# Spatial mixing by seven products of quarters, with x kept in DRAM for the z products and the projection as a stage of its own

## The chip, the core and the metric

One core of one Trainium2 chip runs the whole program. It has five engines with instruction streams of their own: TensorE (PE, matmuls, with weight loads shown as PEld), VectorE (DVE), ScalarE (ACT), GpSimd (POOL) and SyncE (SP, which here issues nearly all transfers). They meet through semaphores. The metric is the time on the device in microseconds (us); a kernel's time is the median of its runs.

## What is computed

x is 2048 x 512. The kernel computes x + s * silu(b), with s an attention over the last 512 keys of a cache and b a gated mixing unit; both take xn, the layer norm of x.

```python
def _A_ref(x, k_cache, v_cache, wq, wo):          # 32 heads of 128, W = 512
    q = (x @ wq)  ... per head
    p = _softmax(q @ k[-W:].T * Dh ** -0.5)
    return concat(p @ v[-W:]) @ wo

def _B_ref(x, w_in, w_sp, b_sp, w_out):           # F = 1376, Fh = 688
    z = _gelu(x @ w_in)
    z1 = z[..., :Fh]
    z2 = _layernorm(z[..., Fh:], axis=-1, eps=1e-5)
    g = einsum("ts,bsf->btf", w_sp, z2) + b_sp[None, :, None]
    return (z1 * g) @ w_out

xn = _layernorm(x)
out = x + _A_ref(xn, ...) * _silu(_B_ref(xn, ...))
```

The mixing is the product of w_sp (2048 x 2048) with the normalised z2 (2048 x 688). Everything is float32.

## The kernel before

A float32 matmul is done as three products of operands split in two: a high part (a cast to the matmul's float32 format, on ACT, called `wh`, `xh`, `z_h` and so on) and the rest (`rest`, L56: whole minus high, on DVE or POOL). `mm3` (L60 to 63) issues high x high, high x low and low x high into one PSUM bank. All of the program is written under a manual schedule: each engine works through its instructions in the order in which the code issues them, and waits in that order.

Rows of x are taken in 16 blocks of 128. The stages follow each other on TensorE:

1. A lead-in: layer norm of x, its transposed and split copy `xT` (L149 to L168), the first products.
2. The attention, 512 steps `t` (L372 to L411), four to each pair of head and quarter of the rows. A step issues scores, the q projection, the product with v and the output product, twelve 512-wide matmuls; each step sends its probabilities to DRAM (`p_dram<-pB`) and four steps' worth come back transposed (`pL<-p_dram`), and loads a piece of the weights (`raw<-wh`). The z1 half of `x @ w_in` and its way to DRAM lie in this stage as well. All these transfers are issued by SP in one order.
3. The z stage (L479 to L491): for each block two 344-wide halves of the z2 product (`z_product`, L448, 12 matmuls each), gelu on ACT and `bn_stats` on DVE (L457, L458), and for every two blocks the norm: aggregation (L464), the inverse root on POOL (`rsqrt`, L68 to L71) and two 688-wide `tensor_scalar` on DVE (L469). `z_split` (L472) makes high and low of z2, the low one on POOL. The 16 blocks of z2 stay in SBUF for the next stage. Within this stage the first w_sp block is loaded and split.
4. The mixing (L632 to L652): for each block i of output rows 16 chunks x 2 halves x 3 matmuls, 344 wide, into `ps_g` (`mix`, L557), while `take` (L541) loads and splits the w_sp pieces of the next blocks, cast on ACT and rest on DVE. Then `gate` (L568) adds the bias and multiplies by gelu of z1 (z1 comes from DRAM, its gelu is L638), `send_u` (L573) turns u in 32 x 32 squares on DVE and sends it through DRAM to get it transposed, `split_u` (L587) splits it, and `project` (L612) multiplies it with w_out, 17 matmuls of 512, one block behind the mixing. Silu, the product with s, the sum with x and the way out are L624 to L627. The last block is flipped by TensorE transposes (`flip_u`) instead of DRAM. ACT loads its tables anew each time it changes between gelu and silu.

The pools overlay each other in SBUF: z2 and the buffers of stages 3 and 4 take the memory of the attention.

## Time and profile before

| what | us |
| --- | --- |
| median of three runs (lowest, highest) | 1837.34 (1837.07, 1839.79) |
| the profiled execution | 1841.09 |
| its span | 1839.2 |
| z products begin, after the span's start | 1478.10 |
| mixing begins | 1536.98 |
| last mixing matmul begins | 1826.29 |

The profile is of one execution. Its page gives the busy time of each engine with its share of the span and the count of instructions; the chain that ended last, by engine; groups of equal instructions with their count, busy time and mean, and behind the last bar the idle time of the engine before them with what ended it; and the transfers with their size and the median time from issue to landing. An answer by windows has, for each stretch, the length, then the busy time of PE, PEld, DVE, ACT and POOL, the granted clock of TensorE, the busy share of the 16 DMA engines, and the GB/s that they moved. A row of the timeline has the start, the time that the row covers, engine, line, operation, output and inputs with their shapes, and the count; in brackets stands how long the engine had been idle, and what released it. The shown time of a single matmul includes its way through the array, so the distance between two starts is what counts.

### The profile page before, as it was taken

The numbers are of one execution on the slowest core, as the hardware profiler recorded it, in microseconds if no ns is written. First come the engines' busy times: TensorE is split into PE (matmuls) and PEld (weight loads), VectorE is DVE, ScalarE is ACT, GpSimd is POOL, SyncE is SP. The second block draws the span as 40 slices with busy tenths as digits, with TensorE's granted clock in tenths as the row PEclk, the third lists the DMA queues.
The fourth block names the chain that finished last, engine by engine and source line by source line (L and its number), as shares of the span: only waits on it lengthen the run. The fifth ranks groups of instructions, "written<-read, shape, count | busy, mean of one in ns | idle before, by whom it ended". The sixth has DMA issues, their size and how long they took to land.

```text
span 1839.2 us, 27426 instructions
## 1 busy us (share of the span) xinstructions
PE 1827.4 (99%) x8828; PEld 1573.1 (86%) x8828; DVE 1356.3 (74%) x2268; ACT 1019.4 (55%) x2188; POOL 873.6 (48%) x703
## 2 busy tenths in 40 slices
PE   8999999999999999999999999999999999999999
PEld 7888888888888888888888888888888999999998
DVE  7688888888888888888888888888888566333433
ACT  3566656666666665666666665665666445343422
POOL 3365555565565565555566555565566244000000
PEclk9999999999999999999999999999999999999999
DMA  5698888888888888888888888888888714554532
GB/s 190 179 234 216 217 219 224 215 218 218 221 214 217 216 219 217 216 214 217 219 224 217 218 216 226 215 218 217 218 215 225 222 65 153 174 184 140 182 120 91
DMA packets 404225, 369.69 MB, mean 201 GB/s; under 512 B 23056, under 2 KB 298768, under 8 KB 404080
## 3 DMA queue, kind: packets, MB, share of 16 engines
q1 hardware_dynamic: 399472, 362.30, 75.1%
q10 hardware_dynamic: 4608, 5.64, 0.9%
q8 instruction: 69, 1.13, 0.3%
q14 instruction: 76, 0.62, 0.1%
HBM read 213.70 MB, written 154.14 MB: 200 GB/s over the span
## 4 chain that ended last, share of the span: by engine, by line
PE 96%; DVE 1%; DMA 1%; ACT 1%; issue 0%; POOL 0%; ACTq 0%; SPq 0%; DVEq 0%; POOLq 0%
PE ps_a L61 14%; PE ps_a L62 14%; PE ps_a L63 14%; PE ps L63 13%; PE ps L61 13%; PE ps L62 13%; PE ps_g L61 4%; PE ps_g L62 4%; PE ps_g L63 4%; PE ps_f L63 1%; PE ps_f L62 1%; PE ps_f L61 1%; DMA z_dram<-z 0%; PE ps_f L621 0%; PE ps L166 0%
## 5 line engine op out<-in xcount | busy, mean ns | idle before, releaser
L57 POOL TENSOR_TENSOR pT_l<-pL,pT_h 128x512 fp32r<-128x512 f32 x507 | 658.6, 1299 | 572.1 <-ACT pT_h L256 526.2
L231 ACT ACTIVATE prob<-ps,nm 128x512 f32<-128x512 f32 x512 | 353.4, 690 | 533.6 <-DVE nm L229 531.5
L283 DVE SCALAR_TENSOR_TENSOR sacc<-ps,sums,sacc 128x512 f32<-128x512 f32 x496 | 370.7, 748 | 170.5 <-PE ps L63 170.4
L239 DVE STREAM_TRANSPOSE pB<-prob 128x512 f32<-128x512 f32 x512 | 359.4, 702 | 1.5 <-ACT pT_h L256 0.8
L229 DVE TENSOR_REDUCE nm<-ps 128x1 f32<-128x512 f32 x512 | 334.8, 654 | 3.6 <-PE ps L63 3.6
L256 ACT CAST pT_h<-pL 128x512 fp32r<-128x512 f32 x512 | 315.8, 617 | 7.6 <-ACT z L198 3.4
L61 PE MATMUL ps<-wh,qT_h 128*128 128x512 f32 x512 | 199.9, 390 | 0.9 <-DVE sacc L281 0.9
L63 PE MATMUL ps<-wh,oT_l 128*128 128x512 f32 x512 | 199.3, 389 | 0.3 <-DVE oT_l L57 0.3
L61 PE MATMUL ps_a<-xh,wh 128*128 128x512 f32 x512 | 199.4, 390 | 0.0
L62 PE MATMUL ps_a<-pT_l,wh 128*128 128x512 f32 x512 | 199.3, 389 | 0.0
L62 PE MATMUL ps_a<-xl,wh 128*128 128x512 f32 x512 | 199.3, 389 | 0.0
L62 PE MATMUL ps<-wl,qT_h 128*128 128x512 f32 x512 | 199.3, 389 | 0.0
L63 PE MATMUL ps_a<-xh,wl 128*128 128x512 f32 x512 | 199.2, 389 | 0.0
L63 PE MATMUL ps<-wh,qT_l 128*128 128x512 f32 x512 | 199.2, 389 | 0.0
L62 PE MATMUL ps<-wl,oT_h 128*128 128x512 f32 x512 | 199.2, 389 | 0.0
L61 PE MATMUL ps_a<-pT_h,wh 128*128 128x512 f32 x512 | 199.2, 389 | 0.0
L63 PE MATMUL ps_a<-pT_h,wl 128*128 128x512 f32 x512 | 199.2, 389 | 0.0
L61 PE MATMUL ps<-wh,oT_h 128*128 128x512 f32 x512 | 199.2, 389 | 0.0
L57 POOL TENSOR_TENSOR wl<-raw,wh 128x512 fp32r<-128x512 f32 (+1 forms) x132 | 169.6, 1286 | 37.0 <-ACT wh L120 37.0
L63 PE MATMUL ps_g<-z_h,xl 128*128 128x344 f32 x512 | 161.8, 316 | 0.0
L61 PE MATMUL ps_g<-z_h,xh 128*128 128x344 f32 x512 | 161.8, 316 | 0.0
L62 PE MATMUL ps_g<-z_l,xh 128*128 128x344 f32 x512 | 161.8, 316 | 0.0
(135 smaller groups left out, 2991.4 us busy)
## 6 DMA issues: line engine op xcount, KB each, us to landing
p_dram<-pB SPq DMA_DIRECT2D x512, 256.0 KB, 3.8
pL<-p_dram SPq DMA_DIRECT2D x512, 256.0 KB, 5.8
raw<-wh SPq DMA_DIRECT2D x128, 256.0 KB, 4.4
xh<-w_sp SPq DMA_DIRECT2D x32, 256.0 KB, 5.8
xl<-w_sp SPq DMA_DIRECT2D x28, 256.0 KB, 5.8
u_dram<-uB SPq DMA_DIRECT2D x15, 384.0 KB, 2.3
uL<-u_dram SPq DMA_DIRECT2D x60, 96.0 KB, 2.1
z_dram<-z ACTq DMA_DIRECT2D x32, 172.0 KB, 2.4
```

Source lines behind the costliest of these rows:

```text
L57: engine.tensor_tensor(lo, whole, hi.bitcast(F32), op=OP.subtract)
L61: nc.tensor.matmul(ps, lh, rh, start=first, stop=False)
L62: nc.tensor.matmul(ps, lh, rl, start=False, stop=False)
L63: nc.tensor.matmul(ps, ll, rh, start=False, stop=last)
L229: nc.vector.tensor_reduce(nm, ps, axis=AX.X, op=OP.max, negate=True)
L231: nc.scalar.activation(prob[t], ps, AF.Exp, bias=nm, accum_out=sums[b][:, j:j + 1])
L239: nc.vector.transpose(pB.rearrange("p (k q) -> p k q", q=Q), prob.pop(t))
L256: nc.scalar.copy(h, p)
L283: nc.vector.scalar_tensor_tensor(sacc[:, i, :], ps, rs, sacc[:, i, :], op0=OP.mult, op1=OP.add)
```

## The change

The mixing is written as a product of 2 x 2 quarters: w_sp is A11, A12, A21, A22 (each 1024 x 1024), z2 is B with row halves 1 and 2 and column halves of 344. Seven products of sums of quarters take the place of eight products of quarters, in the form that shares intermediate sums. For that, the z stage forms seven operands of each chunk: B11, B22, B21 and the sums T1 to T4, each as high and low, in one tile `ops`; the eighth chunk's lie in smaller buffers. Blocks p and p+8 are taken together. The sums of A are formed per pair of row blocks (i, i+8) on POOL. Each of the seven products of a pair takes 8 chunks x 3 matmuls of 344 into a PSUM bank of its own.

For these operands memory is needed that `xT` holds. So from step 32 to step 55 of the attention the blocks of `xT` that the z stage uses after its first two pairs are sent to `x_dram`, 256 KB each, and read back in the z stage (`load_xr`). u of all blocks goes to `u_dram`, and the projection follows the mixing as a loop of 16 blocks.

```diff
+    def keep_x(i, w):
+        g, j = divmod(i, 4)
+        nc.sync.dma_start(x_dram[:, i, w].rearrange("p (c t) -> p c t", c=NC), xT[g][w][:, :, j * P:(j + 1) * P].bitcast(F32))
+    STREAM = [p + a for p in range(2, H8) for a in (0, H8)]
+    KEEP = {32 + 2 * k + w: (i, w) for k, i in enumerate(STREAM) for w in range(2)}
...
             turn(t - 1)
+        if t in KEEP:
+            keep_x(*KEEP[t])
...
-            for k in range(2):
-                nc.vector.tensor_scalar(z[i - 1 + k], z[i - 1 + k], zmv[g][:, k, 0:1], r[:, k:k + 1],
-                                        op0=OP.subtract, op1=OP.mult)
+    T1, B11, B22, B21, T2, T3, T4 = range(7)
+    def z_norm(p, a):
+        for n in range(2):
+            h = z_half(p + a * H8, n)
+            nc.vector.scalar_tensor_tensor(h, h, zmv[p][:, a, 0:1], rz[p][:, a:a + 1].to_broadcast([P, NB]),
+                                           op0=OP.subtract, op1=OP.mult)
+    def whole(k, p):
+        if k == T3:
+            return R[3][:, p % 2 * NB:(p % 2 + 1) * NB]
+        return z_half(*{T1: (p, 0), B11: (p, 1), B22: (p + H8, 0), T2: (p + H8, 0),
+                        B21: (p + H8, 1), T4: (p + H8, 1)}[k])
+    def z_sums(p, which, engine):
+        for to, x0, x1 in which:
+            engine.tensor_tensor(whole(to, p), whole(x0, p), whole(x1, p), op=OP.subtract)
+    EARLY, LATE = ((T3, B22, T1), (T1, T1, B11)), ((T2, B22, T1), (T4, B21, T2))
+    def z_high(c, ks):
+        for k in ks:
+            nc.scalar.copy(op_of(k, c, 0), whole(k, c))
+    def z_low(c, ks, engine):
+        for k in ks:
+            rest(engine, op_of(k, c, 1), whole(k, c), op_of(k, c, 0))
...
+    ops = zp.tile([P, 7, H8 - 1, 2, NB], F32R, name="ops")
+    R = [zm.tile([P, H8 * P], F32, name=f"row{k}") for k in range(4)]
+    A_OF = (11, 12, 21, 22, 21, 11, 12)
+    B_OF = (B11, B21, T3, T4, T2, T1, B22)
+    def sum_a(m):
+        i, q = divmod(m, 7)
+        if i < H8 and q in (2, 4, 5, 6):
...
+            for h in range(2):
+                sl = slice(h * 512, h * 512 + 512)
+                nc.gpsimd.tensor_tensor(r[to][:, sl], r[x0][:, sl], r[x1][:, sl], op=op)
+    def split_a(m, engine=None):
...
+                nc.scalar.copy(hi, r)
+                rest(engine or nc.vector, lo, r, hi)
...
+    for p in range(1, H8):
...
+        for k, (i, n) in enumerate(order):
+            if p > 1:
+                z_product(i, n)
+            z_gelu(i, n)
+            if k == 0:
+                z_sums(p - 1, EARLY, nc.gpsimd)
+                z_high(p - 1, (B11, B22, B21))
+            elif k == 1:
+                z_low(p - 1, (B11, B22, B21), nc.vector)
+                z_sums(p - 1, LATE, nc.gpsimd)
+            else:
+                z_high(p - 1, ((T3, T1), (T2, T4))[k - 2])
+                z_low(p - 1, ((T3, T1), (T2, T4))[k - 2], nc.vector)
...
+            z_root(p, 0, 2)
+            z_norm(p, 0)
+            z_norm(p, 1)
...
+    z_norm(p, 0)
+    z_root(p, 1)
+    z_norm(p, 1)
+    z_high(p, (B11, B21, B22))
+    z_sums(p, EARLY, nc.vector)
+    z_low(p, (B11, B21, B22), nc.vector)
+    z_sums(p, LATE, nc.vector)
...
+    sum_a(2)
+    split_a(2)
+    z_high(p, (T4, T3))
+    z_low(p, (T4, T3), nc.vector)
+    load_row(0, 22, 3)
+    z_high(p, (T2, T1))
+    z_low(p, (T2, T1), nc.vector)
...
+        product(0, range(H8 - 1))
+        product(1, range(H8 - 1))
+        product(0, (H8 - 1,))
+        product(1, (H8 - 1,))
+        for m in range(M):
+            if m > 1:
+                product(m)
+            sum_a(m + 3)
+            if m:
+                split_a(m + 2)
+                outputs(m - 1)
...
+        for j in range(NT - 1):
+            project(j, M + j)
+            if j == 0:
+                outputs(M - 1)
+            split_u(j + 1)
+            load_u(j + 2)
+            load_sx(j + 2)
+            finish(j, M + j)
```

`outputs` adds the products' banks with the bias, multiplies by the gelu of z1 (`z1h`) and turns and sends u: about ten 344-wide DVE instructions and eight transposes for each pair of row blocks. `load_row` loads a quarter row of w_sp (512 KB) into one of four buffers; the fourth, `R[3]`, also holds T3 of the z stage until the last pair's is split. `load_u` fetches a block's u in four transfers, `load_sx` its s and x, `finish` is silu, product, sum and way out.

The order of DVE in the z stage, before, for two blocks (`stz` statistics, `mvz` mean and variance, `rz_r` the inverse root):

```order
L458 BN_STATS stz<-z 128x6 x2
L464 BN_AGGR mvz<-stz 128x2
L458 BN_STATS stz<-z 128x6 x2
L464 BN_AGGR mvz<-stz 128x2
L469 TENSOR_SCALAR z<-z,mvz,rz_r 128x688 x2
```

And now, for one pair of blocks (`blk` the halves of z2, `row_17556` the fourth row buffer with T3):

```order
L460 BN_STATS stz<-blk 128x6 x2
L60 TENSOR_TENSOR ops<-blk,ops 128x344 x3
L460 BN_STATS stz<-blk 128x6
L60 TENSOR_TENSOR ops<-row_17556,ops 128x344
L60 TENSOR_TENSOR ops<-blk,ops 128x344
L460 BN_STATS stz<-blk 128x6
L60 TENSOR_TENSOR ops<-blk,ops 128x344 x2
L467 BN_AGGR mvz<-stz 128x2 x2
L475 SCALAR_TENSOR_TENSOR blk<-blk,mvz,rz_r 128x344 x4
```

The rests of z2 have moved from POOL to DVE, seven 344-wide ones for the pair, and stand among the statistics of the pair that follows; the normalisation has become four instructions with a second tensor input.

POOL in the same place, now (first root, then the four differences of the pair):

```order
L73 TENSOR_SCALAR rz_t<-mvz 128x2
L74 TENSOR_TENSOR rz_r<-rz_t,power 128x2
L486 TENSOR_TENSOR row_17556<-blk 128x344
L486 TENSOR_TENSOR blk<-blk 128x344 x3
L60 TENSOR_TENSOR wl_18200<-row_17554,wh_18198 128x512
L60 TENSOR_TENSOR wl_18201<-row_17554,wh_18199 128x512
L73 TENSOR_SCALAR rz_t<-mvz 128x1
```

Before, the root was followed there by the 688-wide rests of z2. The last rows are those of the seventh pair, where two rests of w_sp come ahead of the last pair's root.

DVE behind the last pair's statistics, up to the mixing (`wl_` and `wh_` the splits of w_sp):

```order
L475 SCALAR_TENSOR_TENSOR blk<-blk,mvz,rz_r 128x344 x2
L486 TENSOR_TENSOR row_17556<-blk 128x344
L486 TENSOR_TENSOR blk<-blk 128x344
L60 TENSOR_TENSOR blk<-blk 128x344 x3
L486 TENSOR_TENSOR blk<-blk 128x344 x2
L60 TENSOR_TENSOR wl_18262<-row_17555,wh_18260 128x512
L60 TENSOR_TENSOR wl_18263<-row_17555,wh_18261 128x512
L60 TENSOR_TENSOR raw<-blk,raw 128x344
L60 TENSOR_TENSOR blk<-row_17556,blk 128x344
L60 TENSOR_TENSOR raw<-blk,raw 128x344 x2
L60 TENSOR_TENSOR wl_18172<-row_17556,wh_18170 128x512
L60 TENSOR_TENSOR wl_18173<-row_17556,wh_18171 128x512
```

`row_17556` is read for T3 by the ninth row from the top of this piece, and by the last two it holds the fourth quarter row of w_sp. Before, the mixing of a block needed only the pieces of one w_sp block, split in the z stage.

More of the change, by code (lines that the diff above doesn't have):

```diff
@@ L417, in mixer_kernel, with load_xr, z_half @@
     z1_out(NT - 1, 1, ps)
+    zst, zmv, rz, zps, xr, zbuf = {}, {}, {}, {}, {}, {}
+    def load_xr(i):
+        xr[i] = []
+        for w in range(2):
+            xr[i].append(rawp.tile([P, D], F32R, name="raw"))
+            nc.sync.dma_start(xr[i][w].bitcast(F32), x_dram[:, i, w])
+    def z_half(i, n):
+        if (i, n) not in zbuf:
+            if i % H8 == 0:
+                zbuf[i, n] = rawp.tile([P, 512], F32, name="raw")[:, :NB]
+            else:
+                zbuf[i, n] = zm.tile([P, HW], F32, name="blk", bufs=11)[:, :NB]
+        return zbuf[i, n]
@@ new lines, in z_product, with z_gelu @@
+    def z_product(i, n):
+        ps = zps[i, n] = ((ps_step.tile([P, 512], F32, name="ps_3") if i < H8 else
+                           ps_acc.tile([P, 512], F32, name="ps_a"))[:, :NB])
+        g, j = divmod(i, 4)
+        for c in range(NC):
+            x2 = (tuple(t[:, c, j * P:(j + 1) * P] for t in xT[g]) if i % H8 < 2 else
+                  tuple(t[:, c * P:(c + 1) * P] for t in xr[i]))
+            mm3(ps, c == 0, c == NC - 1, x2, cols(wt[("w", 2 + n), c], 0, NB))
+    def z_gelu(i, n):
+        if i not in zst:
+            zst[i] = stats.tile([P, 2, 6], F32, name="stz")
+        h = z_half(i, n)
+        nc.scalar.activation(h, zps.pop((i, n)), AF.Gelu_apprx_tanh)
+        nc.vector.bn_stats(zst[i][:, n, :], h)
```

415 lines of the change are left out of this document (217 added, 198 removed).

## The prediction

> **What bounds the kernel now.** I read the page first (busy shares, chain of waits), then busy time by windows, then the timeline of TensorE at the seams of the stages.
>
> ```profile
> span 1839.2 us, 27426 instructions
> PE 1827.4 (99%) x8828; PEld 1573.1 (86%) x8828; DVE 1356.3 (74%) x2268; ACT 1019.4 (55%) x2188; POOL 873.6 (48%) x703
> PE 96%; DVE 1%; DMA 1%; ACT 1%; issue 0%; POOL 0%; ACTq 0%; SPq 0%; DVEq 0%; POOLq 0%
> 100.00:800.00 700.00, 700.00 (x3090) 579.83 (x3089) 581.94 (x966) 427.74 (x965) 414.13 (x322) 1.00 0.87 218
> 1500.00:1550.00 50.00, 50.00 (x328) 50.00 (x327) 33.99 (x54) 26.84 (x49) 30.95 (x29) 1.00 0.27 88
> 1550.00:1600.00 50.00, 50.00 (x312) 48.67 (x311) 21.15 (x36) 18.68 (x25) 0.00 (x0) 1.00 0.64 210
> ```
>
> TensorE sets the time in every stage: no window has a gap, and the granted clock (the column after the five engines) is 1.00. So matmuls taken out pay in full as long as the other engines and the transfers keep up. The windows say how near they are: in the attention the transfers hold 0.87 of the DMA engines; in the z stage (1500 to 1550) DVE is busy 34 of 50 us and POOL 31; in the mixing (1550 to 1600) DVE 21 and POOL none. The change shifts work on all three.
>
> ```profile
> 1478.10 0.32 PE L61 MATMUL ps_a<-wh,xh 128*128 128x344 f32 x1
> 1536.98 0.32 PE L61 MATMUL ps_g<-z_h,xh 128*128 128x344 f32 x1
> 1540.66 0.32 PE L61 MATMUL ps_g<-z_h,xh 128*128 128x344 f32 x1
> 1826.29 0.32 PE L63 MATMUL ps_g<-z_h,xl 128*128 128x344 f32 x1
> 1827.37 0.39 PE L61 MATMUL ps_f<-wo_h,xh 128*128 128x512 f32 x1
> 1828.06 0.39 PE L61 MATMUL ps_f<-wo_h,xh 128*128 128x512 f32 x1
> ```
>
> The z products begin at 1478.10 and the mixing at 1536.98: 384 matmuls in 58.88 us, 0.1533 each. The two ps_g rows 3.68 us apart (24 matmuls) give the same. The ps_f rows, three matmuls apart, give 0.23 for a 512-wide one.
>
> **Matmuls removed.** The mixing had 16 x 16 x 2 x 3 = 1536; seven products of eight chunks for eight row pairs are 8 x 7 x 8 x 3 = 1344. 192 x 0.1533 = **-29.4 us**. The z stage keeps its 384, the projection its 16 blocks; six transposes go (1826.45 to the end is now 12.75 us, beside 14 projections of 17 x 0.23 inside; after, 15 x 3.9 and a tail of some 8.2): **-0.6**. All else hidden, that is 1837.3 - 30.0 = 1807.3.
>
> **The z stage.** Per pair p (blocks p and p+8) TensorE needs 48 x 0.1533 = 7.36 us. DVE had four bn_stats, two aggregations, two 688-wide normalisations per pair; it now has four bn_stats, two aggregations, four normalisations as two-input instructions and seven 344-wide rests, while POOL trades its two 688-wide rests for four 344-wide differences.
>
> ```profile
> L458 DVE BATCH_NORM_STATS2 stz<-z 128x6 f32<-128x344 f32 x32 | 15.9, 512 | 15.6 <-ACT z L457 15.1
> L464 DVE BATCH_NORM_AGGREGATE mvz<-stz 128x2 f32<-128x12 f32 x16 | 3.3, 209 | 0.5
> L570 DVE SCALAR_TENSOR_TENSOR u<-ps_g,bsp,z 128x344 f32<-128x344 f32 x32 | 17.0, 572 | 113.5 <-PE ps_g L63 113.5
> 1477.12 2.21 DVE L57 TENSOR_TENSOR wl<-raw,wh 128x344 fp32r<-128x344 f32 x5
> 1497.87 0.92 DVE L458 BATCH_NORM_STATS2 stz<-z 128x6 f32<-128x344 f32 x2
> 1472.80 0.93 POOL L57 TENSOR_TENSOR wl<-raw,wh 128x344 fp32r<-128x344 f32 x1 [6.65 <-ACT wh L120]
> 1487.00 0.22 POOL L70 TENSOR_SCALAR rz_t<-mvz 128x2 f32<-128x2 f32 x1 [13.27 <-DVE mvz L464]
> 1487.30 0.71 POOL L71 TENSOR_TENSOR rz_r<-rz_t,power 128x2 f32<-128x2 f32 x1
> 1488.05 1.19 DVE L469 TENSOR_SCALAR z<-z,mvz,rz_r 128x688 f32<-128x688 f32 x2 [1.14 <-POOL rz_r L71]
> ```
>
> DVE per pair: statistics 4 x 0.46 = 1.84, rests 7 x 0.44 = 3.09, aggregations 0.42, the wait for the root on POOL 1.14, normalisations 4 x (0.44, the subtract of that width, to 0.57, the gate from PSUM; I take 0.52) = 2.1. Together **8.6**, above TensorE's 7.36 before anything collides. POOL has 4 x 0.93 + 0.93 = 4.65, which would fit beside it, were the two independent. The trace says they are not:
>
> ```profile
> 1495.34 1.69 POOL L57 TENSOR_TENSOR z_l<-z,z_h 128x688 fp32r<-128x688 f32 x1
> 1495.41 2.54 DVE L469 TENSOR_SCALAR z<-z,mvz,rz_r 128x688 f32<-128x688 f32 x2 [1.14 <-POOL rz_r L71]
> 9.99 0.93 DVE L57 TENSOR_TENSOR pT_l<-pL,pT_h 128x344 fp32r<-128x344 f32 x2
> 15.28 1.70 DVE L57 TENSOR_TENSOR wl<-pL,wh 128x344 fp32r<-128x344 f32 x2 [0.51 <-ACT wh L120]
> 15.70 2.06 POOL L57 TENSOR_TENSOR wl<-pL,wh 128x344 fp32r<-128x344 f32 x2
> ```
>
> The pair of L469 that took 1.19 alone took 2.54 behind a POOL subtract of 1.69; two DVE subtracts that took 0.93 alone took 1.70 beside POOL's. The loser waits for the rest of the other's instruction. Rests and normalisations (11 of 17 DVE instructions) are of that kind, so POOL's 3.72 of differences can only lie under DVE's statistics (1.84); the root's wait is POOL's own. Period: 8.6 + 3.7 - 1.84 = **10.5**; bounds 8.6 (no collision) and 12.3 (no cover). [...]
>
> From 1478.10: pair 1's products end at 14.7 (its gelu must wait for them, as its buffers lie where the transposed x was), its normalisation at about 24 (25.7 with collisions), that of pair 6 five periods on, at 67 (78).
>
> **The start of the mixing.** Behind that stand, on DVE, pair 7's statistics, root twice (2.3), norms, two w_sp rests, then its own six differences, seven rests and more w_sp rests.
>
> ```profile
> L57 DVE TENSOR_TENSOR xl<-xh 128x512 fp32r<-128x512 f32 x33 | 21.1, 683 | 7.1 <-ACT xh L549 7.1
> L57 POOL TENSOR_TENSOR xl<-raw_z,xh 128x512 fp32r<-128x512 f32 x4 | 5.2, 1292 | 0.0
> L549 ACT CAST xh<-xh 128x512 fp32r<-128x512 f32 x33 | 18.7, 615 | 1.4 <-DMA xh<-w_out 1.4
> xh<-w_sp SPq DMA_DIRECT2D x32, 256.0 KB, 5.8
> ```
>
> TensorE can hide some under products 0 and 1, whose first seven chunks come early. But product 3 needs the fourth w_sp row, and its load waits on SP until DVE has done the rest of pair 7's T3, since that operand lies in the row's buffer. DVE up to there: 1.84 + 3.09 + 1.37 + 0.42 + 2.1 + 2.3 = 11.1; six differences and five rests 4.9; the half-rows' rests 1.37: normalisation of pair 6 + 16.5 to 17.3. Then the load (I take 4 of the 5.8; 512 KB on an idle queue), cast 0.62, rest 0.68: +21.5 to 22. POOL's last four differences and its two half-row rests (2 x 1.29) can add 5. Product 3 so starts at 67 + 21.5 = 88 (78 + 26.5 = 105), where TensorE alone would be at 58.9 + 3 x 3.68 = 69.9. **Lost: 18 without collisions, 35 with**; I take 35 (31 to 39), as the rows above show the collision for just these forms.
>
> **The rest of the mixing.** A row pair takes 7 x 3.68 = 25.8 us on TensorE. DVE: 14 rests x 0.68 = 9.5, some ten 344-wide additions and gates x 0.5 to 0.57, eight transposes: 16 to 18. POOL: 8 x 1.29 = 10.3. Even excluding each other, 9.5 + 10.3 is under 25.8. **0**; the cover is three sets of splits, two products ahead.
>
> **Saving x.** 24 transfers of 256 KB join SP's queue, one per attention step from 32 to 55, and return in the z stage (0.27 of the DMA engines taken there).
>
> ```profile
> p_dram<-pB SPq DMA_DIRECT2D x512, 256.0 KB, 3.8
> pL<-p_dram SPq DMA_DIRECT2D x512, 256.0 KB, 5.8
> raw<-wh SPq DMA_DIRECT2D x128, 256.0 KB, 4.4
> uL<-u_dram SPq DMA_DIRECT2D x60, 96.0 KB, 2.1
> ```
>
> A step of twelve 512-wide matmuls is 2.73 us and moves 218 GB/s at 0.87, so 262,144 bytes want about 1.05 us of the engines (218/0.87 = 250 GB/s) against 0.36 free: for 24 steps up to 16 us of transfers pile up. They delay p_dram and pL, which have slack of some steps. Bounds 0 and 9 us; I take **+2**, as the queue also holds weight loads that may slip.
>
> **The projection on its own.** Silu now comes without the table switches, off the path before too. At the seam, weights, outputs and the first u block pass DVE behind the last products: **+2.4** (0 to 5). Per block SP moves 384 + 512 + 256 KB, 1.18 MB in 3.9 us: 302 GB/s, against 210/0.64 = 328 at full. u is loaded two blocks ahead when its buffer comes free: landing 2.1, four issues, cast and rests about 5.2 + 2.1 for two periods of 3.9. At a landing of 3 or more it binds: **+2** (0 to 9).
>
> **Sum**: -29.4 - 0.6 + 35 + 2 + 2.4 + 2 = +11.4. The profiled execution took 1841.09 for its span of 1839.2, and the span alone lies 1.9 above the median of the runs, 1837.34; all terms are differences, so I add them to the median: 1848.7, say **1849**.
>
> **Rivals.**
> - *No exclusion between POOL's differences and DVE*: lost 18 in place of 35, and x saved free: -30.0 + 18 + 2.4 + 2 = -7.6 to -5.6: about 1831. For it: L458 ran at its own time beside POOL, and the trace has no 344-wide normalisation. Against it: the 1.70 and 2.54. It ends faster; the sign turns at a loss of about 24.
> - *Everything hidden*: 1807 to 1815. Against it: DVE's 8.6 against 7.36 alone costs 9.
> - *Saving x fills the queue*: with 9 in place of 2, and the projection bound by transfers (+9): about 1860.
> - *A slower clock after pauses.* TensorE would pause for 3 us in each pair.
>
> ```profile
> 10.00:20.00 10.00, 7.79 (x38) 6.79 (x38) 6.28 (x12) 2.94 (x7) 4.01 (x6) 0.84 1.05 393
> ```
>
> Where it paused, at the start, the clock was 0.84. At that, 7.36 becomes 8.8, still under 10.5; only the first products of the mixing would pay, 1 to 4 us: 1852. [...]
>
> **Chances.** Forecast (1840 to 1859) 0.55, no exclusion 0.21, full queues 0.13, clock 0.07, all hidden 0.04. Range **1830 to 1862**: 0.04 and part of the second lie below, 0.06 above. This kernel's times can tell about 0.2% (3.7 us) from nothing. Faster by more: most of the second, the fifth, a sliver of the first, 0.24; same 0.07; slower 0.69.
>
> **What would show it.** Right: in the z stage pairs some 10.5 us apart, subtracts on DVE of 0.8 to 1.4 beside POOL's; TensorE idle by some 35 us between 1478 and 1585, the last wait before the fourth product being the row's load; then products 3.68 apart. Wrong: pairs at 8.6 or less, subtracts at 0.44, or gaps in the attention between steps 32 and 60.

## The result, and the profile after

The changed kernel takes 1866.21 us (median of 4 runs, 1863.36 to 1868.53), the kernel before 1837.61 on the same chip (4 runs, 1837.07 to 1839.79). The ratio is 1.0153, 95% interval 1.0135 to 1.0170: slower, by 1.5%. The prediction said slower, by 11.4 us; it is 28.6 (27.5 between the spans of the two profiles). 1866 lies above the range.

The page of the changed kernel, its busy shares and the shares of the chain that ended last:

```profile
span 1866.7 us, 27811 instructions
PE 1823.3 (98%) x8630; PEld 1559.1 (84%) x8630; DVE 1495.7 (80%) x2496; ACT 1030.9 (55%) x2271; POOL 977.4 (52%) x784
PE 92%; DVE 3%; DMA 3%; ACT 1%; issue 1%; SPq 0%; POOL 0%; ACTq 0%; DVEq 0%; POOLq 0%
```

TensorE has 198 records fewer, as the 192 matmuls and six transposes ask. But its busy time fell by 4.1 us in place of 30: matmuls at a lower clock or a wider spacing count as busy too (from 1574.0 to 1578.7 it is busy for all 4.70 us at a granted 0.62). In the chain that ended last TensorE holds 92%, where it held 96%: the end now hangs, by these rounded shares for some 75 us more, on DVE, on transfers and on issue.

Windows through the z stage and the mixing (columns as before):

```profile
1520.00:1540.00 20.00, 19.86 (x125) 19.32 (x124) 16.79 (x35) 9.34 (x23) 10.39 (x12) 1.00 0.38 128
1540.00:1560.00 20.00, 4.67 (x22) 3.94 (x21) 16.80 (x34) 10.97 (x26) 11.10 (x13) 0.67 0.00 0
1560.00:1580.00 20.00, 16.20 (x69) 14.91 (x67) 15.34 (x26) 5.33 (x12) 8.54 (x14) 0.73 0.19 61
1600.00:1650.00 50.00, 50.00 (x319) 50.00 (x319) 41.55 (x63) 19.78 (x37) 22.63 (x16) 1.00 0.44 141
```

From 1520 to 1560 DVE is busy 16.8 of each 20 us, and what it stands idle it waits for the root and the gelu; between 1540 and 1560 TensorE has little to do, and until 1580 it runs at 0.7 of its clock. The last window looks perfect, 50.00 of 50 at full clock, and yet hides a loss: 319 matmuls in 50 us are one in 0.157, where the kernel before had 328 and 0.1533.

The timeline of TensorE in the changed kernel: first mixing matmul, the first of product 3, two rows 24 matmuls apart (3.78 us) behind it, and the seam to the projection.

```profile
1555.64 0.65 PE L64 MATMUL pm<-ops,wh 128*128 128x344 f32 x1 [13.33 <-ACT wh L553]
1579.34 0.43 PE L64 MATMUL pm<-ops,wh 128*128 128x344 f32 x1 [0.23 <-ACT wh L553]
1583.26 0.32 PE L64 MATMUL pm<-ops,wh 128*128 128x344 f32 x1
1587.04 0.32 PE L64 MATMUL pm<-ops,wh 128*128 128x344 f32 x1
1785.92 0.79 PE L64 MATMUL pm<-ops 128*128 128x512 f32 x1 [4.23 <-ACT ops L738]
1788.96 0.80 PE L66 MATMUL pm<-ops 128*128 128x512 f32 x1 [1.82 <-DVE ops L60]
```

The z products begin at 1478.74. Counted from there (T0), since T0 lies anywhere from 1473.9 to 1479.6 in the runs of this kernel and its edits, the time divides so. "No loss" is the 361.1 us that the kernel before took from its T0 to its end, less 30.0 for the work taken out.

| stretch | no loss | forecast | measured |
| --- | --- | --- | --- |
| start of the span to T0 | 1478.1 | 1480.1 | 1478.7 |
| T0 to product 3 | 69.9 | 104.9 | 100.6 |
| product 3 to the last mixing matmul (1781.38) | 194.9 | 194.9 | 202.0 |
| from there to the end | 66.3 | 70.7 | 85.3 |

The forecast was 4.3 us too high for the start of the mixing and 1.4 too high for saving x; it was 7.1 too low in the mixing and 14.6 too low behind it: 16.0 in all. That the two terms priced too high hid 5.7 of the 21.7 that were missing is luck. These two stretches are what the experiments had to settle, beside the start, which is the largest loss and may have come out right for a wrong reason.

### The profile page after: what moved, and what is told of

It reads as the page before. It is cut to its first block, busy times and chain, and to the rows that moved or that the text cites. A ratio compares the mean times of both kernels' runs of the same rounds, so it can differ in the third digit from the quotient of the medians.

```text
span 1866.7 us, 27811 instructions
## 1 busy us (share of the span) xinstructions
PE 1823.3 (98%) x8630; PEld 1559.1 (84%) x8630; DVE 1495.7 (80%) x2496; ACT 1030.9 (55%) x2271; POOL 977.4 (52%) x784
## 4 chain that ended last, share of the span: by engine, by line
PE 92%; DVE 3%; DMA 3%; ACT 1%; issue 1%; SPq 0%; POOL 0%; ACTq 0%; DVEq 0%; POOLq 0%
PE ps L64 13%; PE ps L66 13%; PE ps_a L66 13%; PE ps_a L64 13%; PE ps L65 13%; PE ps_a L65 13%; PE pm L66 4%; PE pm L65 4%; PE pm L64 4%; DVE ops L60 1%; DMA ops<-u_dram 1%; DMA raw<-x_dram 1%; DVE wl L60 1%; DMA z_dram<-z 0%; PE ps L188 0%
## 5 line engine op out<-in xcount | busy, mean ns | idle before, releaser
L285 DVE SCALAR_TENSOR_TENSOR sacc<-ps,sums,sacc 128x512 f32<-128x512 f32 x496 | 370.7, 748 | 169.2 <-PE ps L66 168.9
L545 POOL TENSOR_TENSOR row<-row,row 128x512 f32<-128x512 f32 x64 | 100.9, 1605 | 103.8 <-DMA row<-w_sp 69.5
L221 DVE SCALAR_TENSOR_TENSOR qT_l<-ps_a,qT_h 128x512 fp32r<-128x512 f32 x128 | 88.6, 692 | 67.7 <-ACT qT_h L220 67.7
L64 PE MATMUL pm<-ops,wh 128*128 128x344 f32 x392 | 127.5, 325 | 13.6 <-ACT wh L553 13.6
```

Of the source, the lines that this page charges most:

```text
L64: nc.tensor.matmul(ps, lh, rh, start=first, stop=False)
L221: nc.vector.scalar_tensor_tensor(lo, ps, SCALE, hi.bitcast(F32), op0=OP.mult, op1=OP.subtract)
L285: nc.vector.scalar_tensor_tensor(sacc[:, i, :], ps, rs, sacc[:, i, :], op0=OP.mult, op1=OP.add)
L545: nc.gpsimd.tensor_tensor(r[to][:, sl], r[x0][:, sl], r[x1][:, sl], op=op)
```

## The experiments

All are the changed kernel with an edit, if nothing else is said, and are compared by stretches from T0, since total times contain the spread ahead of it. What a stretch repeats to: where an edit leaves the start alone, product 3 comes between T0 + 100.4 and 101.0, and where it leaves the mixing's end and the projection alone (the first three runs below), these take 83.9 to 85.6.

### What sets the start of the mixing

**POOL's differences left out** (pairs 0 to 6):

```diff
             if k == 0:
-                z_sums(p - 1, EARLY, nc.gpsimd)
                 z_high(p - 1, (B11, B22, B21))
...
-                z_sums(p - 1, LATE, nc.gpsimd)
```

> Leaves out the four differences that POOL forms for each of the pairs 0 to 6 in the z stage (the operands T1 to T4 of these pairs are then plain blocks, so the output is not the reference's); everything else is kept. Theory (POOL's differences shut DVE's two-input instructions out): a pair takes 8.0 to 8.7 us in place of 10.0 (root to root on POOL), DVE's 344-wide rests fall from 0.69 to about 0.44 and the normalisations from 0.64 to about 0.51, the last pair's root comes 7 to 10 us earlier, and the whole is 6 to 10 us shorter. Rival (DVE's own work sets the pace, the pairs of slow instructions are chance): the pair stays at 10.0 and the time within 2 us.

The roots of pairs 1 and 6 and DVE's rests, first of the changed kernel, then of this run:

```profile
1501.50 0.71 POOL L74 TENSOR_TENSOR rz_r<-rz_t,power 128x2 f32<-128x2 f32 x1
1551.43 0.71 POOL L74 TENSOR_TENSOR rz_r<-rz_t,power 128x2 f32<-128x2 f32 x1
L60 DVE TENSOR_TENSOR ops<-blk,ops 128x344 fp32r<-128x344 f32 x36 | 23.4, 688 | 0.0
```

```profile
1500.40 0.71 POOL L74 TENSOR_TENSOR rz_r<-rz_t,power 128x2 f32<-128x2 f32 x1
1543.40 0.71 POOL L74 TENSOR_TENSOR rz_r<-rz_t,power 128x2 f32<-128x2 f32 x1
L60 DVE TENSOR_TENSOR ops<-blk,ops 128x344 fp32r<-128x344 f32 x36 | 17.8, 536 | 0.0
L475 DVE SCALAR_TENSOR_TENSOR blk<-blk,mvz,rz_r 128x344 f32<-128x344 f32 x28 | 16.4, 645 | 7.9 <-POOL rz_r L74 7.8
```

Five pairs take 49.9 us with POOL's work and 43.0 without: 10.0 and 8.60 a pair. A rest of unchanged size and operands takes 536 ns in place of 688. Product 3 comes at T0 + 91.1, 9.5 earlier. So the two engines do hold each other up, and the rival "no exclusion" is out; but POOL's differences cost 9.5 us, not the 17 between the prediction's two cases. The normalisations take as long without them (645 ns; 644 in the changed kernel, shown below), against the expectation of some 0.51 us: the differences read what the normalisations write and so come behind them, and of a pair's instructions only the rests are slowed by them (the statistics at 1517.25, wholly within a row of POOL's differences, took 0.51 us, and those at 1519.59, behind it, 0.51 too). The larger part of the 30.7 stays, 21.2: DVE's own work, the load of the fourth row, and POOL's work on w_sp, which this run keeps. The run took 1860.44.

**The normalisation as an instruction without a second tensor:**

```diff
-            nc.vector.scalar_tensor_tensor(h, h, zmv[p][:, a, 0:1], rz[p][:, a:a + 1].to_broadcast([P, NB]),
-                                           op0=OP.subtract, op1=OP.mult)
+            nc.vector.tensor_scalar(h, h, zmv[p][:, a, 0:1], rz[p][:, a:a + 1], op0=OP.subtract, op1=OP.mult)
```

> The normalisation as a tensor_scalar with two per-partition scalars in place of a scalar_tensor_tensor with a broadcast second input. Theory (DVE's two-input work and POOL's differences take turns and set the pace): a normalisation falls from 0.51 to about 0.30 (1.19 for 2 x 688 in the kernel before), a pair from 10.0 to 9.1 to 9.4, and the end by 4 to 6 us. Rival (the pair's pace is set by POOL's chain of root, differences and casts): the pair stays within 0.2 of 10.0.

The group in the changed kernel, then in this run:

```profile
L475 DVE SCALAR_TENSOR_TENSOR blk<-blk,mvz,rz_r 128x344 f32<-128x344 f32 x28 | 16.4, 644 | 7.8 <-POOL rz_r L74 7.8
```

```profile
L475 DVE TENSOR_SCALAR blk<-blk,mvz,rz_r 128x344 f32<-128x344 f32 x28 | 12.9, 521 | 7.9 <-POOL rz_r L74 7.8
```

The pairs take 9.51, a little above the 9.1 to 9.4 expected, and product 3 comes at T0 + 97.5: 3.1 us won by a form that computes the same. Four times the 0.12 us that an instruction got shorter is the 0.5 that a pair gains, so it is the instruction itself that is cheaper, no collision that went. The run took 1859.83; its span is 8.7 us shorter, but 4.7 of these lie ahead of T0, which this edit cannot reach: a reason to compare stretches.

**The clock kept up** by 78 + 36 matmuls whose results nobody reads:

```diff
+    dz = ps_step.tile([P, 512], F32, name="ps_3")
+    for _ in range(78):
+        nc.tensor.matmul(dz[:, :NB], op_of(B11, 0, 0)[:, :P], op_of(B11, 0, 0), start=True, stop=True)
...
+        bank(2)
+        for _ in range(36):
+            nc.tensor.matmul(banks[2][:, :NB], op_of(B11, 0, 0)[:, :P], op_of(B11, 0, 0), start=True, stop=True)
         product(0, (H8 - 1,))
```

> Adds 78 idle-filling matmuls (344 wide, their result unused) behind the last z product and 36 more ahead of the eighth chunks of products 0 and 1. Theory (the first products run at half clock because TensorE paused): the first products of the mixing follow each other at about 0.158 in place of 0.287, the granted clock between 1540 and 1580 rises from 0.67 and 0.73 to above 0.95, and the fourth product starts up to 6.5 us earlier. Rival (the chain on DVE and the load of the fourth row set the fourth product's start, and the slow matmuls only fill its wait): it starts at the same place to 1.5 us, with the wait ahead of it grown by what the products saved.

Two windows and the start of product 3 in this run:

```profile
1540.00:1560.00 20.00, 17.35 (x108) 16.78 (x107) 16.79 (x34) 11.21 (x26) 10.40 (x13) 0.97 0.00 1
1560.00:1580.00 20.00, 19.10 (x106) 18.81 (x104) 15.60 (x26) 4.63 (x11) 8.29 (x14) 0.86 0.15 46
1580.53 0.43 PE L64 MATMUL pm<-ops,wh 128*128 128x344 f32 x1 [1.43 <-ACT wh L553]
```

The clock rises from 0.67 and 0.73 to 0.97 and 0.86, DVE's busy time stays, and product 3 starts at T0 + 100.9. The slow matmuls at the start cost nothing: DVE's chain sets this start, not TensorE. Its last link here is the load of the fourth row: issued at 1575.98, when DVE is done with T3, landed at 1579.78, and the cast (`wh`) waits for it alone. In the changed kernel it was issued at 1575.04, and its cast, at 1578.67, is put down to TensorE's products 0 and 1, which end at 1578.65, most of their last stretch at half speed (0.287 apart up to 1577.46): there the two links come out together.

### The spacing in the mixing

**A pause in the kernel before.** One matmul ahead of the mixing of block 5 waits for a POOL instruction; all else is the kernel before.

```diff
+            if i == 5:
+                s3 = us[3, "x"][0]
+                nc.gpsimd.tensor_tensor(gap[:, :64], s3[:, :64], s3[:, 64:128], op=OP.subtract)
...
+                nc.tensor.matmul(us[5][0][:64, :64], gap[:, :64], gap[:, :64], start=True, stop=True)
```

> The kernel before, with one pause of TensorE of some 3 us ahead of the mixing of block 5 (a small matmul that waits for a POOL subtract of the third block's product with s). Theory A (a lead that the sequencer loses in a pause and wins back under 512-wide matmuls): the 96 matmuls of block 5 stand 0.158 apart, those behind the next projection 0.153 again, and the time grows by the pause, its slow clock if any, and 0.4 us. Theory B (a state after a pause): 0.158 from there to the end, some 960 matmuls x 0.0044 = 4.2 us beside the pause. Theory C (operands): 0.153 throughout.

```profile
1630.16 0.24 PE L641 MATMUL ps_g<-gap 128*64 128x64 f32 x1 [2.52 <-POOL gap L639]
1636.12 0.32 PE L61 MATMUL ps_g<-z_h,xh 128*128 128x344 f32 x1
1639.90 0.32 PE L61 MATMUL ps_g<-z_h,xh 128*128 128x344 f32 x1
1647.00 0.39 PE L61 MATMUL ps_f<-wo_h,xh 128*128 128x512 f32 x1
1651.36 0.32 PE L61 MATMUL ps_g<-z_h,xh 128*128 128x344 f32 x1
1655.04 0.32 PE L61 MATMUL ps_g<-z_h,xh 128*128 128x344 f32 x1
```

(This run took 1847.43. Narrow stands for 344 columns, wide for 512.) After a pause of 2.5 us 24 narrow matmuls take 3.78 us, as in the mixing of the changed kernel; behind the next projection, 17 matmuls of 512, they take 3.68 again. Operands and code are the same. So a pause alone slows narrow matmuls, by 2.7%, until wide ones have run.

The z stage of the changed kernel shows the same without an edit. Up to 1496.98 its 344-wide products stand 0.1533 apart; then one waits 2.0 us for a block of x, and from there on 24 take 3.79, with the same split of w_in (`wh`) as moving data:

```profile
1499.33 0.39 PE L64 MATMUL ps_a<-wh,raw 128*128 128x344 f32 x1 [2.03 <-DMA raw<-x_dram]
1503.63 0.32 PE L64 MATMUL ps<-wh,raw 128*128 128x344 f32 x1
1507.42 0.32 PE L64 MATMUL ps_a<-wh,raw 128*128 128x344 f32 x1
```

**Wide matmuls into the changed mixing**: 24 ahead of products 16 and 37, then 96 with changing weights ahead of product 16.

```diff
+            if m in (16, 37):
+                bank(m)
+                w = ring[m % 3][0][0]
+                for _ in range(24):
+                    nc.tensor.matmul(banks[m], w[:, :P], w, start=True, stop=True)
```

> Adds 24 matmuls of 512 columns (result unused) ahead of products 16 and 37 of the mixing. In the mixing of the changed kernel 344-wide matmuls stand 0.1577 apart, 0.1533 before TensorE's first pause at 1497. Theory A (the sequencer needs 0.158 for a pair of weight load and matmul, and the 0.153 of before is lived from a lead that wider matmuls rebuild): behind each block of 512-wide ones the spacing is 0.153 for some tens to some hundreds of matmuls, then 0.158 again. Theory B (a state that TensorE keeps after a pause) and theory C (where the operands lie): 0.158 throughout. The added blocks themselves are 2 x 24 x 0.228 = 10.9 us; A gives up to 3.3 of them back, B and C nothing.

> 96 matmuls of 512 columns with changing weights (result unused) ahead of product 16 of the mixing, where 24 with the same weights left the spacing of the 344-wide ones behind them at 0.158, while in the kernel before 17 of them had brought it back to 0.153. If it was their number or the repeated weights: 0.153 behind the block, for 50 matmuls or more. If the mixing itself holds 0.158 (where the operands lie, or the waits that stand at every twelfth matmul): 0.158 from the first one behind it. The time grows by 96 x 0.228 = 21.9 us, less up to 4.

In both the spacing stays at 0.158 behind the wide ones, so neither brought 0.153 back (1870.51 and 1884.57 us). The pause is not all of it.

**Probes.** Behind wide matmuls stand 48 narrow ones that read one fixed place as moving data, with nothing to wait for: in the first run the start of a w_sp split, an operand's high part, its low part; then places 0, 32, 64, 96, 128 and 192 bytes into a w_sp split; then the order 128, 0, 96, 0, 64, 0.

```diff
+                for o in (32, 0, 24, 0, 16, 0):
+                    for k in range(16):
+                        nc.tensor.matmul(banks[m], w[k // 4 % 2][:, k % 4 * P:k % 4 * P + P], w[k % 2], start=True, stop=True)
+                    for k in range(48):
+                        nc.tensor.matmul(banks[m][:, :NB], w[k // 4 % 2][:, k % 4 * P:k % 4 * P + P], w[0][:, o:o + NB], start=True, stop=True)
```

> Ahead of product 16 of the mixing, three times: 24 matmuls of 512 columns, then 48 of 344 columns without a wait among them (results unused); the 344 moving columns are, in turn, a split of w_sp, the high part of an operand in the tile of operands (its start a multiple of 64 bytes) and its low part (32 bytes further). If what holds the mixing at 0.158 is where its operands lie: 0.153 in the first run of 48, 0.158 in the third, perhaps in the second. If it is the waits at every twelfth matmul: 0.153 in all three, 0.158 again in the product behind. If it is a state that wider matmuls do not lift here: 0.158 in all three. The time grows by 72 x 0.228 + 144 x 0.155 = 38.7 us.

> Ahead of product 16 of the mixing, six times: 16 matmuls of 512 columns, then 48 of 344 (results unused) with one and the same tile as moving data, read from 0, 32, 64, 96, 128 and 192 bytes behind its start (the tile's own address is a multiple of 128 bytes). If the start of the moving data within 128 bytes sets the spacing: 0.153 at 0 and 128, 0.158 at 32 and 96, 0.160 at 64 and 192. If it is the tile of operands as such (its place in memory, or other engines' traffic there): 0.153 at all six. The time grows by 96 x 0.228 + 288 x 0.156 = 66.8 us.

> As the run with the offsets, but in the order 128, 0, 96, 0, 64, 0 bytes. If the start of the moving data decides: 0.153 in the second, fourth and sixth run of 48, and 0.157, 0.158, 0.156 in the first, third and fifth. If the order decides (a lead or state that the first run uses up): 0.153 in the first alone.

The third run's rows where 48 at 128 bytes begin, the wide ones behind them, 48 at 0, and the wide ones behind those:

```profile
1633.99 0.79 PE L775 MATMUL pm<-wh 128*128 128x344 f32 x4
1641.54 0.39 PE L773 MATMUL pm<-wh 128*128 128x512 f32 x1
1645.17 0.78 PE L775 MATMUL pm<-wh 128*128 128x344 f32 x4
1652.53 0.39 PE L773 MATMUL pm<-wh 128*128 128x512 f32 x1
```

7.55 us and 7.36. In all three runs the place decides, whatever the order: 7.36 at 0 bytes, 7.52, 7.49, 7.56, 7.55 and 7.68 at the others; 7.57 for the operand's high part and 7.68 for its low. The second run's theory, 128 bytes as fast as 0, failed with its 7.55, and so did its rival, 0.153 at all six.

**The place, in the mixing itself.** Products 3 to 48 read operands that lie at one chosen place modulo 256 bytes; the last of the three runs also has 24 wide matmuls ahead of product 16.

```diff
+        def rhs(m, k, c, w):
+            if not 2 < m < 49:
+                return op_of(k, c, w)
+            j = min(((k * 7 + min(c, 6)) * 2 + w) // 8 * 8 + 1, 97)
+            return ops[:, j // 14, j // 2 % 7, 1]
```

> Products 3 to 48 of the mixing (1104 matmuls) read as moving data only those operands of the tile that begin at a multiple of 16 x 1376 = 43 x 512 bytes from its start, in place of their own (so the output is not the sum of products that the reference asks for; count, width, weights and banks of the matmuls stay). Theory (where the moving data begin decides the 0.1575 spacing): these products run at 0.1533, 24 matmuls in 3.68 us, product 3 to product 49 in 169.3 us, and the mixing gets some 4.7 us shorter than the 202.0 of the changed kernel. Rival (the pause ahead of the mixing, or something else of this stage such as seven banks in place of two, keeps the 0.1577): 24 matmuls stay at 3.78, product 3 to product 49 at 174.

> The same with operands that begin 8 x 1376 = 43 x 256 bytes, times an odd number, from the tile's start (again not the products asked for). Theory that any start at a multiple of 256 bytes is fast: as in the run with 512, 24 matmuls in 3.68 us. Theory that it must be 512: between 3.74 and 3.84, as at 128 and 192 bytes. If the start does not matter at all: 3.78, like the run with 512.

> The built program puts the operand tile at byte 94496 of each partition, 32 above a multiple of 256, and the w_sp splits of the probes 128 above one. So the probes' 0, 32, 64, 96, 128 and 192 bytes are the places 128, 160, 192, 224, 0 and 64 modulo 256 (7.36, 7.52, 7.49, 7.56, 7.55, 7.68 per 48), and the operands of the two runs before both lay at 32 (7.68). Here products 3 to 48 read as moving data only operands that lie at 128 modulo 256 (again not the products asked for), and 24 wide matmuls stand ahead of product 16. Theory (the place modulo 256 decides): 24 matmuls in 3.68 us, in products 17 to 48 at least; from product 17 to 49 some 768 matmuls in 117.8 us. If a pause also keeps the spacing high until wide matmuls come, products 4 to 15 stay at 3.78 or so and only those behind the wide ones show 3.68. Rival (the place in the tile is not what holds the mixing): 3.78 or more throughout, 121.0.

In the first two 24 matmuls took 3.84 in every product from 6 to 48, 0.1600 each: slower than the kernel's own operands, where the theory had 3.68 and its rival 3.78 (the second run had 3.74 to 3.84 for the case that only multiples of 512 are fast, which the first run refutes). That led to the addresses: the tile itself lies 32 bytes above a multiple of 256, so both runs had chosen the place 32. The third run, ahead of the wide matmuls, at them, and behind them (each pair of rows is 24 matmuls apart):

```profile
1600.25 0.32 PE L64 MATMUL pm<-ops,wh 128*128 128x344 f32 x1
1604.03 0.32 PE L64 MATMUL pm<-ops,wh 128*128 128x344 f32 x1
...
1627.70 5.64 PE L778 MATMUL pm<-wh 128*128 128x512 f32 x24
...
1680.10 0.32 PE L64 MATMUL pm<-ops,wh 128*128 128x344 f32 x1
1683.78 0.32 PE L64 MATMUL pm<-ops,wh 128*128 128x344 f32 x1
```

3.78 and 3.68: the good place alone does not bring 0.1533, and at the kernel's own places the wide matmuls alone did not either. Both together do. (The three runs took 1869.51, 1867.08 and 1867.03; only their mixing is compared.) That accounts for the spacing: a pause raises it to 0.1577 until wide matmuls come, and at each of the five other places that were read behind wide ones it stays between 0.156 and 0.160 even then. The kernel before has neither: no pause of TensorE in these stages, wide matmuls of the projection in every block, and rows of z2 that step by 1536 bytes, six times 256, from a place at 128 in the built program. The changed kernel has both, and either alone would hold it near 0.1577: the pause at its start, a projection moved out of the mixing, and operands that step by 1376 bytes through eight places.

### The seam and the projection

**Loads of s and x left out** for blocks 2 to 15, and **a third buffer for u** with all transfers kept:

```diff
-            load_sx(j + 2)
```

```diff
+        uset.append([space(T4, o, n) for o, n in ((0, 768), (768, 768), (1536, 640))])
...
+                load_u(2)
...
-            load_u(j + 2)
+            load_u(j + 3)
```

> Leaves out the loads of s and x for the projection's blocks 2 to 15 (the last steps then work on what lies in the buffers, so the output is not the reference's). In the changed kernel 14 blocks from 1794.2 took about 10 us longer than 14 x 3.87 and the tail. Theory (bandwidth: 1.18 MB a block near what the DMA engines carry): with 0.66 MB a block nearly all of it goes, 7 to 10 us. Rival (the chain through two u buffers: product ends, load, cast, rests, next product but one): landing of u falls from 2.7 to about 2, and 2 to 5 us go, with TensorE still waiting for the cast of u at some blocks.

> A third buffer for u in the projection (in the space of an operand that is done), loads three blocks ahead; the same traffic. Theory (bandwidth): at most 3 us of the 10 go, the DMA share stays at 0.87 or rises, and the waits for the cast stay. Rival (the chain through two buffers): 6 to 10 us go and blocks stand 3.87 apart.

The same 40 us, and the loads of u between 1795 and 1850, in the changed kernel, without s and x, and with three buffers:

```profile
1795.00:1835.00 40.00, 37.91 (x158) 28.55 (x157) 25.54 (x46) 12.51 (x19) 0.00 (x0) 1.00 0.84 262
ops<-u_dram SPq DMA_DIRECT2D x48, 96.0 KB, 2.7
```

```profile
1795.00:1835.00 40.00, 39.11 (x164) 29.74 (x163) 26.12 (x47) 14.06 (x20) 0.00 (x0) 1.00 0.53 159
ops<-u_dram SPq DMA_DIRECT2D x48, 96.0 KB, 2.4
```

```profile
1795.00:1835.00 40.00, 39.60 (x167) 30.43 (x166) 26.66 (x50) 13.35 (x19) 0.00 (x0) 1.00 0.92 272
ops<-u_dram SPq DMA_DIRECT2D x44, 96.0 KB, 4.5
```

From the first projection matmul to the end it takes 80.8, 73.8 and 74.4 us. With three buffers the load lands later (4.5 us) on fuller DMA engines (0.92), and yet TensorE waits less. So the bytes are not the bound; the chain through two buffers is: free, issue, land, split, multiply. Lighter transfers shorten that chain, a third buffer takes it off the path. The totals, 1856.61 and 1856.70, contain a T0 that was 4.9 and 4.4 us early.

**u loaded ahead of w_out**, and w_out split in the order of its chunks:

```diff
-                load_wo()
                 load_u(0)
+                load_u(1)
+                load_wo()
```

> Order alone: the loads of the first two u blocks go ahead of the fourteen loads of w_out on SP, these go by chunks, and the split of the first u stands ahead of the second half of w_out's. In the changed kernel TensorE stood 4.4 us between the last product and the first projection, then 1.8 more, and ten matmuls ran at half clock (2 us). Theory (SP's queue of w_out issues, 8.4 us, holds back u): 4 to 7 us go. Rival (the end of the mixing on DVE, outputs and rests, holds the seam): under 2 us.

SP's queue in the changed kernel:

```profile
1772.99 8.38 SPq L708 DMA_DIRECT2D row<-w_out  x14
1781.47 1.74 SPq L723 DMA_DIRECT2D ops<-u_dram  x4
```

A miss: the first matmul comes 0.8 us earlier, then waits 3.1 us for w_out; seam and projection take 87.3 in place of 85.3, and the run 1870.78. The 14 transfers of w_out hold SP for 8.38 us, 0.6 each, and the four of u stand behind them; turned round, w_out is late instead. What is short, it seems, is SP's time to issue, 10.1 us for both, after w_out's place in the row buffers comes free. The rival's number (under 2 us) came out; its cause, DVE's end of the mixing, did not: the first version below keeps DVE's work there, and its seam is 0.7 us.

### Put together

The first version has the `tensor_scalar`, three u buffers, and w_out laid out in DRAM in the z stage, so that nine transfers load it in place of 14, early, into T3's memory. The second also starts the first three products earlier, in the seventh pair, and keeps the last T3 in PSUM so that product 3's row loads early.

```diff
+        if p == 5:
+            for n in range(2):
+                nc.sync.dma_start(wo_dram[64 * n:64 * n + 64], w_out[n * NB:n * NB + 320, :].rearrange("(k r) d -> r k d", r=64))
```

```diff
+        if k == T3 and p == H8 - 1:
+            return last_t3
...
+        if p == H8 - 2:
+            for i, n in ((p + 1, 0), (p + 1 + H8, 0), (p + 1, 1), (p + 1 + H8, 1)):
+                z_product(i, n)
+            new_ring(3, 1)
+            split_a(0)
```

> Three changes that the runs asked for: the normalisation as tensor_scalar, three u buffers in the projection, and w_out laid out in DRAM in the z stage and loaded with 9 in place of 14 transfers, into the space of T3, one product earlier. Theory (the losses at z, at the seam and in the projection are separate): -8.7 and -11.8 add up, and the seam gives 3 to 6 us: 1840 to 1843. Rival (what one gives the next stage takes back, since DVE or SP is behind anyway): 1846 or more.

> The same, and the start of the mixing put otherwise: the splits of the first two w_sp rows move ahead of the last two pairs' ends on DVE, the difference for product 2 and its split ahead of the last norm, T3 of the last pair lies in PSUM so that the fourth row can be loaded at once, and TensorE takes products 0 to 2 as far as their operands are there. Theory (the start is held by the order of DVE's chain and by the row's load): the fourth product starts 3 to 8 us earlier than in the version without it, and the whole ends at 1833 to 1839, at the kernel before or under it. Rival (DVE's work in sum is the bound there, order changes nothing): within 2 us of the version without it.

They take 1853.87 (4 runs, 1849.57 to 1855.71; ratio to the kernel before 1.0068, 1.0052 to 1.0085) and 1852.17 (5 runs, 1846.83 to 1856.53; 1.0062, 1.0043 to 1.0081). The first gains 13.1 us from T0 to the end; its seam is 0.7 us, with 3.9 us of SP's time for w_out in place of 8.4 (the order of the splits changed too). Its 1840 to 1843 was missed because -8.7 and -11.8 were whole spans that held early T0s of 4.7 and 4.4 us; from T0 the single gains were 4.0 and 7.4, and with 3.8 at the seam they make 15.2. In the second the projection takes 68.7, but product 3 still starts at T0 + 99.6, where 3 to 8 us less than the first version's 97.5 were expected: with the row load out of the way (issued at 1557.80) TensorE waits 6.4 us for DVE's rests of the last pair and 1.5 for a cast behind DVE's differences. So that load was not all that held it, and the start is 2.1 us later than in the first version. Neither version reaches the kernel before.

## Why the prediction was right or wrong

- **Matmuls removed, -29.4, and transposes, -0.6: not refuted.** 198 records fewer. No run measures the 30.0 by itself; the losses below are counted against it.
- **The z stage, a pair in 10.5: right within 5%.** It is 10.0, and the bound without collisions, 8.6, was met to the second digit (8.60). Mis-sized was the collision: 1.9 forecast, 1.4 measured. I had counted the normalisations among the instructions that collide; they take 644 ns with POOL's differences and 645 without. One place in the changed kernel shows how it looks, a POOL instruction of two differences and DVE's two rests:

```profile
1517.07 2.22 POOL L486 TENSOR_TENSOR blk<-blk 128x344 f32<-128x344 f32 x2 [0.97 <-ACT blk L459]
1517.68 0.82 DVE L60 TENSOR_TENSOR ops<-row,ops 128x344 fp32r<-128x344 f32 x1
1518.42 1.25 DVE L60 TENSOR_TENSOR ops<-blk,ops 128x344 fp32r<-128x344 f32 x1
```

  The two rests, 0.44 each alone by the prediction's rows, take 2.0. That is 1.1 more, and when the first of them began, POOL's row had 1.61 still to run; in the kernel before it was 1.35 more (2.54 - 1.19), with 1.62 to run. That a DVE instruction waits out the rest of POOL's, on which the 1.9 was built, was my estimate from such rows: they come near it, and no run shows it by itself. What a run does show is that without POOL's differences a pair took 1.4 us less (10.0 against 8.60).
- **The start of the mixing, +35: 30.7.** Without POOL's differences I had 18, the run had 21.2 (91.1 - 69.9); with them 35 against 30.7. The kind of cause was right, DVE's chain. From the normalisation of pair 6 to product 3 I had 21.5 without them (my own terms give 21.8 to 22.6) and 26.5 with; it is 25.6 and 27.2, so the collision was priced too high in the pairs and at the end, and what DVE has to do at the end too low. The last link, as I put it, was the load of the fourth row behind T3. It is that where the clock was kept up, in the two z stage runs and in the first combined version; but the second combined version took it out and started no earlier for it, so other work of DVE was due as late.
- **The rest of the mixing, 0: wrong, +7.1.** I asked whether the other engines keep up, and they do (no wait over 0.7 us from product 3 on). I took the 0.1533 of the kernel before as a property of the matmul. It was one of its operands' places and of what ran before: 1271 matmuls at 0.1577 cost 5.6 us more, and products 3 and 5, with waits of 0.7 and 0.2 us for splits of w_sp, the other 1.5 (4.86 and 4.27 us in place of 3.78).
- **Saving x, +2: nothing.** The groups of ACT's probabilities up to steps 31 and 93 (the three numbers are durations in ns, then the first start and the last end), before and then after:

```profile
L231 ACT ACTIVATE prob<-ps,nm x31: 682/689/691, 47.2 to 128.2; 128x512 f32<-128x512 f32 x31
L231 ACT ACTIVATE prob<-ps,nm x93: 682/690/692, 47.2 to 297.1; 128x512 f32<-128x512 f32 x93
```

```profile
L233 ACT ACTIVATE prob<-ps,nm x31: 681/688/692, 48.7 to 128.8; 128x512 f32<-128x512 f32 x31
L233 ACT ACTIVATE prob<-ps,nm x93: 680/689/692, 48.7 to 297.7; 128x512 f32<-128x512 f32 x93
```

  From the end of step 31 to that of step 93 it takes 168.9 us in both, with all 24 transfers among them. Half of the rival "full queues" falls with that.
- **The seam, +2.4, and the projection, +2: wrong, 19.0 together, more than the upper ends of both.** At the seam I looked at DVE and not at SP's time to issue; 4.5 us pass before the first matmul, 1.8 more inside the first block, and ten matmuls at half clock behind the two (rows 0.43 apart, a granted 0.50 from 1789.0 to 1792.5); some 10 us go in the blocks behind. There I named the chain through two buffers, with the landing time from which it binds, 3 us, and then priced it at 2; it binds at 2.7 already, and my own sum (two periods of 3.9 less 5.2) gives 2.6. The third buffer gave 6.4 back.
- **A slower clock: there, and free at the start.** The clock did fall, to 0.67, and warming it changed nothing, since TensorE waited for DVE anyway. I had asked what pauses cost at the clock; what they left was a wider spacing for the rest of the stage, which the operands' places would have held there in any case. The 3 us of pause in each pair did not come: in the z stage of the changed kernel TensorE waited once for 2.0 us and once for 0.2, and the clock stayed at 1.00 (1499 to 1540). Behind the pause of 13.33 us ahead of the mixing the rows stand 0.287 apart at a granted 0.50 (1556 to 1563), and half clock lasts from 1555.64 to 1564.08, 8.4 us with one wait of 2.0 in it. In the kernel before, a pause of 2.5 us was enough for rows 0.287 apart, and they ended at 1634.39, 4.2 us after the first matmul.

## What to carry to other kernels

Before pricing a matmul by a row of the old kernel, compare where its moving data begin and what runs ahead of it: packing operands tightly, or a pause with no wide matmuls behind it, cost 3% here, in a stage in which no engine shows a wait. Where work moves to another engine, add up that engine's whole chain to the first use of its results, collisions included, and count the queue's time to issue at a seam as work like any other.

## What the hardware showed that was not expected

- Behind wide matmuls a narrow float32 matmul (344 wide, own weights) came every 0.1533 us when its moving data began 128 bytes above a multiple of 256; 0.1567 at 160, 0.1560 at 192, 0.1575 at 224, 0.1573 at 0, 0.1600 at 64. At 32 it was 0.1600 too, in the mixing, with no wide ones ahead. Why is open; the place 96 was not measured by itself.
- After a pause of 2.5 us about twelve matmuls ran 0.287 apart, and the narrow ones behind them 0.1577, for as long as no 512-wide ones came; a wait of 2.0 us in the z stage brought the 0.1577 without the 0.287. What wide matmuls do to end this is open.
- A version with operands padded to good places wasn't tried: even 352 columns in place of 344 want 3 KB more in each partition, where the tile's neighbour leaves 32 bytes, and would step by 1408 bytes, which puts only every second operand at 128.
